# A new recorded order for the first part of a Performer-attention and FNet-mixing kernel: other engines and other PSUM banks for the same instructions

## The chip, the core and the metric

The kernel runs on one core of one Trainium2 chip. The core has five engines, each with an instruction queue that is worked off strictly in order: TensorE (PE) for matmuls and transposes, VectorE (DVE), ScalarE (ACT), GpSimd (POOL), and SyncE (SP), which here issues nearly all DMA transfers. They meet through semaphores: an instruction at the head of a queue waits until its semaphores have reached their values, and everything behind it on that engine waits with it. The metric is the time of one execution in microseconds (us); lower is better.

## The reference, cut to what matters

Inputs: q, k, v of 8 batches x 8 heads x 576 positions x 64, omega (128 x 64), and two weight matrices, 512 x 2048 and 2048 x 512 (given as 64-bit floats).

```
phi(x) = exp(x @ omega.T - |x|^2/2 - max(...)) / sqrt(128)      # per position, 128 features
kv     = sum over positions of phi(k) (x) v ;  z = sum of phi(k)
attn   = (phi(q) @ kv) / (phi(q) @ z + 1e-6)                     # 8 x 576 x 512 after joining the heads
u      = attn + Re(FFT over positions and channels of attn)
out    = u + relu(norm(u) @ w1) @ w2                             # norm: mean 0, variance 1 per row
```

## The kernel before, in words

**Two parts.** The first part does attention, the Fourier mixing, the narrowing of the weights to 32 bits, and the first 512 of the 4608 rows of the final two-matrix block ("plain" rows). The second part does the other 4096 rows in 8 blocks, with a Strassen-like scheme of 7 x 7 products (lines 1495, 1646 and 1892). The change touches the first part alone.

**The steps of the first part.** Work is written as Python generators that yield `Step` objects, one per group of instructions on one engine.

- `attn(n)` (32 of them, one for a pair of heads): `transposed` (L564) turns k and q on PE in groups of 4, 4 and 1 blocks into a PSUM bank each, `evicted` copies each group to SBUF on ACT (L580) or DVE (L578); `pairs_of` (L658) projects on omega into a pair of banks, for 4, 1 and 4 blocks; `softmax` takes row maxima on DVE (L601) and exponentials on ACT (L618); the KV step (L692) sums k features times v, `keep` copies the result (L706 DVE or L708 ACT); the q features are turned (L564 again, evicted the same way); the ND step (L739, L747) multiplies them by kv; then the quotient is formed on DVE (L756, L757, L768), or the last of it on ACT (L764, ten instructions in place of one).
- `mix(b)` (8, one per batch): `folds` adds and subtracts halves on DVE or POOL (L795 to L831), PE multiplies by the tables (L851, L861, L901, L912), `residual` and `summed` add the result to x (L945 to L963), which goes to DRAM through SP.
- `narrow(i)` (32): one 128 x 512 piece of weights, on ACT or POOL (L491, L489), then DVE (L494 to L501), then POOL or DVE (L507).
- `plain_of(j)` (4): L1167 and L1190 on PE, with `hidden` (L1151 DVE or L1153 ACT) between; `w2_parts` prepares sums of the second weight matrix on POOL or DVE (L1332).
- `warm` issues six dummy matmuls (L535) that depend on no load; `first` turns omega (L543), which is loaded through ACT's queue (L447).

**What sets the order.** `Listing.run` holds the next step of every generator. It does not decide anything itself here: the string `PICKS` has one character per step. `picked` reads a character as a number and splits it by 36: the remainder says which of the waiting steps comes next, the quotient which of the engines that the step allows does it (capital letters are the second engine). The string `BANKS` has one digit per PSUM request: the bank, or the first of a pair. The steps are emitted in that sequence, and each engine's queue is that sequence cut to the engine:

```
            other, n = next(picks, (None, None))
            for item in todo if n is None else [todo[n]]:
                got = self.start(*item[2:], other, item[0] + item[2].bias if n is None else None)
...
        if self.taken < len(self.given):
            i = int(self.given[self.taken])
            return i, max(t, *self.banks[i : i + n])
```

The cost figures in the steps are a plan's and have no influence on the chip once a character is given for each step. `PICKS2` and `BANKS2` do the same for the second part.

## Time and profile before

| what | value |
|---|---|
| median of 3 runs (lowest to highest) | 1133.14 us (1130.63 to 1134.68) |
| the profiled execution's own time | 1134.51 us |
| its span in the trace | 1132.7 us |
| granted TensorE clock, mean | 1.00 |
| last instruction of the first part on PE, first of the second part | 421.6 us |
| PE busy | 1116.3 us, 99% |
| DVE, ACT, POOL busy | 77%, 48%, 38% |

How to read it: a busy PE is one with a matmul somewhere in its pipeline, so short waits hide in its 99%. What a wait costs is seen better from one matmul's start to the next one's. In the views that list waits, `ACT e L618 <- DVE nmx L601` means that ACT stood idle ahead of the exponentials of L618 until DVE's maxima of L601 were there. A time window is given as start:end from the span's start.

### The profile page before, as it was taken

The numbers are of one execution on the slowest core, as the hardware profiler recorded it, in microseconds if no ns is written. First come the engines' busy times: TensorE is split into PE (matmuls) and PEld (weight loads), VectorE is DVE, ScalarE is ACT, GpSimd is POOL, SyncE is SP. The second block draws the span as 40 slices with busy tenths as digits, with TensorE's granted clock in tenths as the row PEclk, the third lists the DMA queues.
The fourth block names the chain that finished last, engine by engine and source line by source line (L and its number), as shares of the span: only waits on it lengthen the run. The fifth ranks groups of instructions, "written<-read, shape, count | busy, mean of one in ns | idle before, by whom it ended". The sixth has DMA issues, their size and how long they took to land.

```text
span 1132.7 us, 34265 instructions
## 1 busy us (share of the span) xinstructions
PE 1116.3 (99%) x13643; PEld 1040.2 (92%) x13643; DVE 867.6 (77%) x1732; ACT 541.7 (48%) x1644; POOL 428.1 (38%) x438
## 2 busy tenths in 40 slices
PE   8999999999999999999999999999999999999998
PEld 7778888879868778999999999999999999999998
DVE  6999899987576655796787778678678678678666
ACT  7888898856535216614424424424423522522311
POOL 2443443654573214613612710710720630540361
PEclk9999999999999999999999999999999999999999
DMA  7856766565763238797797798797698698798576
GB/s 242 224 177 180 224 181 215 170 206 170 222 196 126 93 92 284 211 314 246 227 339 232 219 329 241 213 326 258 202 323 264 210 281 298 214 268 293 184 223 205
DMA packets 187966, 258.30 MB, mean 228 GB/s; under 512 B 52384, under 2 KB 83360, under 8 KB 187808
## 3 DMA queue, kind: packets, MB, share of 16 engines
q1 hardware_dynamic: 187312, 255.85, 73.1%
q8 instruction: 109, 1.79, 0.7%
q14 instruction: 49, 0.40, 0.1%
q10 hardware_dynamic: 496, 0.26, 0.1%
HBM read 212.27 MB, written 47.97 MB: 230 GB/s over the span
## 4 chain that ended last, share of the span: by engine, by line
PE 89%; DVE 4%; ACT 3%; DMA 2%; issue 1%; SPq 0%; DVEq 0%; ACTq 0%
PE banks L1892 28%; PE banks L1495 28%; PE banks L1167 5%; PE banks L658 5%; PE banks L1190 5%; PE banks L564 4%; PE banks L1646 4%; PE banks L692 3%; PE banks L739 2%; PE banks L901 2%; ACT e L618 1%; PE banks L851 1%; DMA unT<-turned 1%; DVE nmx L601 1%; PE banks L861 1%
## 5 line engine op out<-in xcount | busy, mean ns | idle before, releaser
L1892 PE MATMUL banks<-wl,sums 128*128 128x128 f32 x1792 | 218.9, 275 | 0.7 <-DVE sums L1460 0.7
L1892 PEld LDWEIGHTS banks<-wl,sums 128*128 128x128 f32 x1792 | 209.3, 192 | 1.1 <-DVE sums L1460 0.9
L618 ACT ACTIVATE e<-banks,nmx 128x128 f32<-128x128 f32 x576 | 164.3, 423 | 24.3 <-DVE nmx L601 23.7
L1460 POOL TENSOR_TENSOR hid<-hid 128x512 f32<-128x512 f32 x97 | 127.0, 1314 | 119.1 <-ACT hid L1552 66.5
L1892 PE MATMUL banks<-wl,hid 128*128 128x128 f32 x1344 | 170.6, 275 | 0.6 <-DVE part L1870 0.4
L1892 PEld LDWEIGHTS banks<-wl,hid 128*128 128x128 f32 x1344 | 160.2, 192 | 1.1 <-DVE part L1870 0.6
L601 DVE TENSOR_REDUCE nmx<-banks 128x8 f32<-128x1024 f32 (+1 forms) x96 | 89.4, 952 | 18.3 <-PE banks L658 14.2
L1495 PE MATMUL banks<-rx,wx 128*128 128x128 f32 x672 | 88.8, 275 | 0.0
L1865 ACT ACTIVATE s<-banks 128x128 f32<-128x128 f32 x112 | 30.8, 277 | 113.2 <-PE banks L1892 97.7
L1495 PEld LDWEIGHTS banks<-rx,wx 128*128 128x128 f32 x672 | 81.8, 192 | 0.0
L658 PE MATMUL banks<-om,kqT 64*64 64x128 f32 (+1 forms) x2088 | 78.7, 275 | 2.2 <-ACT kv L708 1.9
L1538 DVE TENSOR_TENSOR hid<-banks,s 128x512 f32<-128x512 f32 x72 | 49.7, 691 | 38.9 <-PE banks L1495 36.9
L658 PEld LDWEIGHTS banks<-om,kqT 64*64 64x64 f32 (+1 forms) x2088 | 64.3, 138 | 13.1 <-issue 3.6
L1870 DVE TENSOR_TENSOR part<-banks,s 128x128 f32<-128x128 f32 x112 | 32.1, 288 | 50.0 <-PE banks L1892 48.8
L1520 ACT ACTIVATE s<-banks 128x512 f32<-128x512 f32 x65 | 38.7, 596 | 59.7 <-PE banks L1495 58.6
L1167 PE MATMUL banks<-unT,w 128*128 128x128 f32 x512 | 65.4, 279 | 1.7 <-DVE qeT L578 1.7
L507 POOL TENSOR_TENSOR w<-w,raw 128x512 f32<-128x512 f32 x28 | 37.7, 1356 | 77.6 <-DVE raw L501 77.6
L1442 DVE CUSTOM_DVE_ANT_0 hid<-banks,s 128x512 f32<-128x512 f32 x63 | 43.6, 692 | 27.5 <-PE banks L1495 25.2
L1167 PEld LDWEIGHTS banks<-unT,w 128*128 128x128 f32 x512 | 60.2, 192 | 4.5 <-issue 2.3
L1460 DVE TENSOR_TENSOR hid<-hid 128x512 f32<-128x512 f32 x91 | 61.1, 712 | 3.8 <-ACT hid L1598 3.8
L1518 DVE TENSOR_TENSOR s<-banks,hid 128x512 f32<-128x512 f32 x70 | 48.4, 691 | 19.0 <-PE banks L1495 16.7
L1941 POOL TENSOR_TENSOR ur<-ur,part 128x512 f32<-128x512 f32 x21 | 26.8, 1281 | 95.4 <-ACT part L1934 91.6
(200 smaller groups left out, 2387.4 us busy)
## 6 DMA issues: line engine op xcount, KB each, us to landing
wl<-w2l SPq DMA_DIRECT2D x392, 256.0 KB
wx<-w1l SPq DMA_DIRECT2D x126, 256.0 KB
raw<-in_moe_w_ch_dram SPq DMA_DIRECT2D x32, 512.0 KB
kq<-in_k_dram SPq DMA_DIRECT2D x32, 288.0 KB
kq<-in_q_dram SPq DMA_DIRECT2D x32, 288.0 KB
vd<-in_v_dram SPq DMA_DIRECT2D x32, 288.0 KB
u<-us SPq DMA_DIRECT2D x36, 256.0 KB
ur<-us SPq DMA_DIRECT2D x36, 256.0 KB
```

Source lines behind the costliest of these rows:

```text
L564: nc.tensor.transpose(ps[:, (j - j0) * 128 : (j - j0 + 1) * 128], src(j), ident[:])
L601: nc.vector.tensor_reduce(nmx[:, :, 0:num], pps[:, :, 0 : MF * num].rearrange("p b (c m) -> p b c m", m=MF), axis=AX.X, op=ALU.max, negate ...
L618: nc.scalar.activation(out=e[:, c + (i if num == 1 else 0), :], in_=pps[:, i, MF * c : MF * c + MF], func=AF.Exp, bias=nmx[:, i, c : c + 1],)
L658: nc.tensor.matmul(pps[cols, c, MF * m : MF * m + MF], lhsT=kqT[rows, j, cols], rhs=om2[rows, :],)
L1167: nc.tensor.matmul(hp[:, 0:TP], lhsT=w1[:, dc, 128 * fc : 128 * fc + 128], rhs=unTs[key][:, dc, :], start=(dc == 0), stop=(dc == NDC - 1),)
L1190: nc.tensor.matmul(yp[:, 0:DM], lhsT=hs[fc][:, 128 * i : 128 * i + 128], rhs=w2[:, fc, :], start=(fc == 0), stop=(fc == NFC - 1),)
L1460: eng.tensor_tensor(out=o, in0=l, in1=r, op=op)
L1495: nc.tensor.matmul(ps[:, P * f : P * f + P].rearrange("f (b q) -> f b q", q=Q), lhsT=left[:, P * f : P * f + P], rhs=right, start=start an ...
L1518: nc.vector.tensor_tensor(out=s[:], in0=ps, in1=cell_of(addend, f, t), op=ALU.add)
L1538: nc.vector.tensor_tensor(out=o, in0=ps, in1=kept[saved][:], op=ALU.add)
L1646: nc.tensor.matmul(cell.rearrange("f t (b q) -> f t b q", q=Q), lhsT=w[:, d, col : col + 128], rhs=right[:, :, d].rearrange("f (t b) q -> ...
L1892: nc.tensor.matmul(ps[:, 0:128], lhsT=left[:, f], rhs=wls[j, i, n][:, f], start=start and f == 0, stop=(f == 3), skip_group_check=True,)
```

## The change

The strings `PICKS` (1853 choices) and `BANKS` (470 requests) of the first part are replaced; no other line is touched.

```
 PICKS = (
-    "40e0f03eafdaegebg3NbcbeefdcOdeccfgdb37ghj0gjj7hlP79aj7ik97i8S7efhjffeHldffiehdjfdOihgihidaKedbhhciff"
...
+    "410ff4bdcegdge0efcgbfcb9eacg38agdahQiRg3gjPihae887ggdhaPg8gbfaahej88khfef9eajih0Pdbkdmebejf8e7b9dea9"
...
 BANKS = (
-    "0102346120164024306243643016204164024320632462014021604606245062345042604670426420340267407231640260"
...
+    "0123460254604623465402560723462040260762407646206124016404267023406214260456274260340265042673502642"
...
```

The instructions are the same in kind and number, apart from those that change engine. Read off the two built programs:

| work | engine before | engine after |
|---|---|---|
| evictions of turned k, q and features (L580 ACT, L578 DVE), instructions | ACT 221, DVE 67 | ACT 232, DVE 56 |
| `keep` (L708 ACT, L706 DVE) | ACT 20, DVE 12 | ACT 26, DVE 6 |
| quotient (L764 ACT, ten each; L768 DVE) | ACT 4, DVE 28 | ACT 9, DVE 23 |
| first step of `narrow` (L491 ACT, L489 POOL) | ACT 24, POOL 8 | ACT 28, POOL 4 |
| `hidden` (L1153 ACT, L1151 DVE) | ACT 44, DVE 20 | ACT 36, DVE 28 |
| first folds (L795) | DVE 11, POOL 5 | DVE 8, POOL 8 |
| sums of `w2_parts` (L1332) | DVE 10, POOL 34 | DVE 18, POOL 26 |

On PE the 498 steps of the first part are the same, in another order. The first rows of PE's queue are, before: dummy matmuls (L535), four transposes of the first k (L564), omega's transpose (L543), five transposes, `pairs_of` for 4 and 1 blocks, four transposes of the second k, `pairs_of` for the last 4 blocks. After: omega's transpose, the dummy matmuls, nine transposes of the first k and q, `pairs_of` for 4, 1 and 4 blocks, nine transposes of the second k and q. PE changes its tiling (whole array, rows, halves, quarters) 167 times before and 173 times after. At the end of the part the last mixing step of the last batch stands ahead of the last eight L1190 steps before, and ahead of the last five after; SP's last store of that batch's rows then stands behind the copy that waits for its mirrored rows (L988). The second part's queues are the same, instruction by instruction.

More of the change, by code (lines that the diff above doesn't have):

```diff
@@ L67 @@
 PICKS = (
-    "40e0f03eafdaegebg3NbcbeefdcOdeccfgdb37ghj0gjj7hlP79aj7ik97i8S7efhjffeHldffiehdjfdOihgihidaKedbhhciff"
-    "ecgOfeejdfdPdeeedgifdffdefd8aiii88jhd8jP8b99i8e8jcddghjgheiifcOcdciieicgPgdefJcdghbkededfgcRbggb79ij"
-    "8hi7hjafN9Haj9gfffeg8eif8hcej1jccc7ehidbhffLigebfbe6766gggfcbjahj9Ofghhjj8dQkkgT6jghff8de6dUjfhbgegh"
-    "cefhafjUf8jgciSjOckkhjakkaeikggjlioklnhSgodoXON7l7l6nnj9icadc97cibf98ejH88a7edhMlhkmjjaQVijihkkfplSm"
-    "okliljjilVaghVhnmljkmpjkhhnmkimlgglmbjpjjQ9d9alafhhdjlaMdjback0j766k7lh4g896ck6gkki77gij5ijhgj6dimni"
@@ L73 @@
-    "3ndjgi6Kc4jldlKikbkaijLhf75dcjlmklk36ci45jciekajkkkk5kihokeaeoLaioNlencidonbSiljjcmjjkboijTUUhgcfkik"
-    "hiflkmeFF99nol5m8jT7naabda89Rbj97ecdl8cjilOgifkQb4acahg57ebbgabgdjkdTkk6eceebb5f9dg4R6ce486ggg6egfhh"
-    "fg4g9egf5cbdhgPRhhcgjhggejigibLmHnbedijj6NOb7biihi9bgihMkaffPa8cijdhbdghbaeibNefffacjicigifi99975ih5"
-    "jgj8699ajfg6g7fgefd65bO6Kalkkgd5jgjikagfldliPJpeoaeeefgdejadgilgScljiii5e65k56kl57k7j67S9lilk9gliih6"
-    "ffkgec4fg4dbgg7fedaiP5gfbheefilddddddeghg9kbfncgghcfkkafkagGngb65p5Hopoj4bhoanbelli68bjjl5b7dlhighhi"
@@ L78 @@
-    "lflhpkgiWomjknmmmkimnjbjhn9jkmFKkfFgedccff6Wf7idUVhi8Th3fogbqp8fgmkeSdjna7ckenoghmnmffnjeo79q6547oa4"
-    "nlkpd7aceonnc8blSVicilbhmjim8fh7SnnIl5mUkfjgfhhfhihg8ghfbS4kjf83j4lllb79jei8mnkblfnmmiolpilOUi9Mh5l5"
-    "pmnaem79jjVmkbblek5iji9a9kffTgjikhiShfgjafhgfigh4g50PPP0ba5Pdh9dghdK77hgfdcbg8OO988jMehefibjjkellfcc"
-    "PcdhQMihfQcffbKCf82b3c98cbcdcd6a299efgddbJaGQQbefLa9ecf74gg986HRgf9idg8kQeheff7be6ff2e5cc8fbcgdKP8f8"
-    "9hN9Lc999bddcHcNb7Oc9effegd7ibhQeQ8haf7ccghhlUikhHW5lWmm5dkMQGM71fS6d1gdb99747ifddhIfdhhdhfdbihgiljn"
@@ L83 @@
-    "gWgijgg93ekKl8kEhIIbT3jjKgkb9k9eTfhkhlje34m49974iG66h68faHe6e7a79982975aI94a39c8cM8b4aa7ab984fge8eLM"
-    "98b86ce8PbFPc9cbe6cKPf3a9b94fIdIQeJKbd876eJPdc5fNb7ffbf9JSS8RiLa4a7gPbajfgg8gdfhg2i2787Hf6OcdIN5d3LH"
-    "accd46ddeKK72dJc7bbaa4bb9a9bc7c0777dghhdf7Bfddebd76ff1fddIe9949438686bc6aca85348dHcG7a5be957b55d1544"
-    "9Gc1F5a9a68446344584584E59189970955888574443113301110"
+    "410ff4bdcegdge0efcgbfcb9eacg38agdahQiRg3gjPihae887ggdhaPg8gbfaahej88khfef9eajih0Pdbkdmebejf8e7b9dea9"
+    "Habc9jb88fjj9hhUhb7hdclMhRh7b7k8Kbcb7cbbbdhdeaebbh78dbbe79iaaeaQccfee9e7hhce8bdMbbdfgcfbhkdf8Mfbecib"
@@ new lines @@
+    "ji9eagSdddjhiagjffedifedjla918jki9ch9ejMggbaeelm6f9bihjdl78hdJjfP9gkhfccbijgfdkbl6d7fae9d7fkfhgideaj"
+    "hbg9efiekjePg6eiciaie9M6dglikhOKMicafbm6ifdejeii9lckkNij7dhijfhabgaecad7ffOba7cdgc8Pcfjdfeibdafcbc7c"
+    "gKiaijgieMbaci9jifgQlbeQfRgibg9hkgkejfhcd0hme7hc4abefi7gdLm8ke9kbabc8bl5hdffahOcjchhef6db5dkiji8c9eO"
+    "O8ame77jgibeeQ8g9cO377hhgikjfcfill9mg7gle9ld7bQlhldcll3e7gfif9d8eTdeedclf8hh8kV8dhcjhejdcaIbfd9fOhG8"
+    "Shb9igfdNg88MddaehfacebfbcbbcPb9bf85aaadGhffhP4h5gea7bhjjhkR88kkk9aeheibchg697ghggc6agaae49ah86geMdb"
@@ new lines @@
+    "akd9fgchfQge9bbMfjiSddckl9hLReifUUibai9fjceOdjebhafi6jhdie7acg9jbMOfc6eb98hf9R6kk489ejeg896eef6c8hgf"
+    "NNfg85lgi7ld8mbhh8hTgh8dgcmeiampjhOld9hmadhi5fdbaONegghiecQikfi5589bgbd9f9ifacfeiadmfhfiihk9NlikkRa9"
+    "4bd4gadcae9fcbiehbdMbfcNcdPbfcefcegdd68M7dcc9hckfKh4fdddhacl9mmi9ijgcafkh85K6fajjdfjgg778iHl7hmghio6"
+    "phNoO6heelh9peeghkgokdhflhfelmgbfek74cfg8lc8m6eNidTicjT3h8eTgaUi7ghhcigRPcoRiigefgj7lfbjU8Wj47efe6i9"
+    "fT4akgdd84khij9fb6achjj7eegf8Ode7gfg4ckfbijbj6nhmmgckf38jlg9lmmbOkd9elgahL9ihWlnkg7mlilmn8enn5abpqId"
@@ new lines @@
+    "mllceiecQjhafkkbkjOie6kgdeTe8dgc0QgcdOOdd4fMFMdbf3bb98GcNOdcg5dbd7aK5RSiNRd7Qc6gf9ddMfbb7K8eLfcbNcae"
+    "aagdfaOdLeON53ebceg9f7JMdcdb4bcKa9a785d78f07e832J7N5e796L5d76eGcI29e6L6cgb6fc7hIge8KJ5Icdb6cabdLc677"
+    "bb677afG5aPIJaffffdOeO6ab455cd9acbc4a8cb8bffaa9e59Lfaj4Hchaijj95abcIgafdQg8PR3heb9bba7eJ76edb397eMdb"
+    "acfafg51fa6c9iaeMhj8iOa6dTT2S6bc5d6666gffbgfabe6gcfHch9Hfab4ffJg9ad1ddbJb7N45f7HaMbc55cH9ddd4cM95747"
+    "a6GNddIab9H0G7454cb44Jafbbbc9a3aMf95geL3dca6gdaQgejj8h19Rc7OPbbe8i8cghcd90g68Mhib19c7eh9Dag7d67i3I0f"
@@ L87 @@
+    "6d8F9fcff9d8G8b90beae49eaffacaa6cb667bb8251343448954798abc83b3F477aaaE98aaa2a7Da9G049b56bbG59387K841"
+    "766438014353154A6392869265903131651442144453022210000"
 )
 BANKS = (
-    "0102346120164024306243643016204164024320632462014021604606245062345042604670426420340267407231640260"
-    "4524016460620240674206206415704602546064320143607264506402346234062732017426042106147026740260462462"
-    "0410652604632452017205467402624060404256174302642060245016745202642016420634520520650162505605260250"
@@ L93 @@
-    "1675602501605204672016204567627450264102316742067460260462045642062637230724672402630145420640106240"
-    "5264023026731602454230412046450416725730620424670121726154305610207453"
+    "0123460254604623465402560723462040260762407646206124016404267023406214260456274260340265042673502642"
+    "0162014246406420140214604630240632456724072360346241064206342064726345723046013240364270164206402420"
+    "6406152470426701457043762462042040642630271432602464206723146702604236240120164261426416243615246214"
@@ L95 @@
+    "5671362416124606245234026540742360642360152706432637026426130724062042150634527240612345042623452042"
+    "6064502670425142605246430264670645107243620642601453726140152606706420"
 )
```

## The prediction, made before the run

> **What bounds the kernel now.** I read the stretches of the span first. Columns: length, then busy time of PE, its weight loads, DVE, ACT and POOL, then clock, DMA share and rate.

> ```profile
> 0.00:27.00 27.00, 23.67 (x375) 20.38 (x375) 17.74 (x29) 19.51 (x68) 6.83 (x14) 1.00 0.79 239
> 27.00:72.00 45.00, 42.67 (x943) 36.25 (x943) 42.51 (x90) 41.10 (x153) 18.06 (x17) 1.00 0.66 186
> 72.00:117.00 45.00, 42.70 (x969) 36.80 (x970) 41.96 (x99) 37.91 (x134) 17.06 (x19) 1.00 0.71 213
> 117.00:172.00 55.00, 53.13 (x1228) 47.17 (x1227) 51.15 (x106) 48.51 (x179) 25.00 (x22) 1.00 0.68 197
> 172.00:222.00 50.00, 50.00 (x1120) 43.27 (x1122) 47.35 (x106) 44.09 (x156) 24.16 (x24) 1.00 0.62 194
> ```

> From 27 to 222 us DVE is busy 93 to 95% of the time and ACT 84 to 91%: both run a step behind PE. Next, PE's starts. I took the spacing of each kind of matmul from the timeline (112 ns for L1167, 109 for transposes, 429 for L1190), and for each of the 498 PE steps the shortest usual time to the next one: 0.437 us for four transposes, 0.874 for four blocks of projection, 1.024 for KV, 1.166 for ND, 1.92 for each of L851's, 1.41 or 0.71 for a mixing step, 0.893 for L1167's group, 1.719 for L1190's, some 0.125 for a change of tiling. With the dummy matmuls this adds up to 394.4 us. The second part starts at 421.6, so PE loses 27.2 us. Where: a step with 10 us of PE work ahead of it starts 4.9 us late, with 20 us 6.1, with 60 us 11.5, with 100 us 16.5, with 200 us 22.1. The second part (711 us) is L1495 and L1892 at 112 ns each, with under 2 us lost in all; its queues are unchanged. So the prize is at most 27 us, and 16 of it lie in the first 117 us.

> Then the chain of work that ended last, between 40 and 100 us (start, length, what):

> ```profile
> 45.61 4.63 ACT e L618 x18
> ...
> 54.04 1.24 DVE nmx L601
> ...
> 57.16 2.14 ACT x L764 x10
> ...
> 71.49 4.97 DMA raw<-in_moe_w_ch_dram
> ...
> 87.97 2.63 ACT e L618 x10
> ...
> 90.83 2.06 ACT e L618 x8
> ```

> The chain leaves PE for ACT's exponentials and DVE's maxima: there PE is fed just in time. Last, the timeline of PE in the opening:

> ```profile
> 1.04 2.93 PE L535 MATMUL banks<-ur 128*128 128x128 f32 x12 [1.04 <-DVE ur L449]
> 3.96 1.08 PE L564 MATMUL banks<-ident,kq 128*128 128x128 f32 x4
> 4.84 0.42 PE L543 MATMUL banks<-ident,om 128*128 128x128 f32 x1
> 5.05 1.04 PE L564 MATMUL banks<-ident,kq 128*128 128x128 f32 x5
> 6.02 1.39 PE L658 MATMUL banks<-om,kqT 64*128 64x128 f32 x20
> 9.52 0.66 PE L564 MATMUL banks<-ident,kq 128*128 128x128 f32 x4 [2.11 <-DMA kq<-in_k_dram]
> ```

> The dummies fill the time until k lands, at 213 ns each; matmuls are spaced by half that from 5.7 us on, where the granted clock becomes 1.00. PE waits once, 2.1 us for the second k.

> **The change, part by part.** All sums are against the profiled execution (span 1132.7, its own time 1134.5); the median of the runs shown is 1133.1, and I carry the differences over to that.

> *Opening: a loss.* Omega's transpose now heads PE's queue and waits for its load, whose last semaphore update is at 4.02 us; the twelve dummy matmuls (six calls) stand behind it. Omega turned at 4.05, dummies 12 x 0.213 = 2.56 until 6.83, nine transposes at 0.213 until 8.75 (3.96 to 6.0 before). ACT's first eviction goes from 5.08 to 7.93. I followed the new queues by hand from there. First projection 8.75 to 9.65, its maxima on DVE 9.98 to 11.1 (1.13 each), then the maxima of the other two groups to 12.6, two evictions at 0.6 to 13.8. ACT has exponentials from 11.25 (0.25 each): 4, 2, 4 and 4, to 14.75. The first KV step needs the last of these: 14.9, against 12.98 before, with 0.2 us more PE work done ahead of it: 1.7 us later. The second k (landed 9.47) costs no wait now. Walked on to 18 us of PE work, ACT never stands idle, PE has lost 7.2 us, and the deficit against before is 1.2 us, since before also waits there. Bounds: 0.3 (the clock is granted as early as before, and the transposes take half the time) and 2.5 (cold through the projections too). I take 1.2, where the walk ends. [...]

> *Tiling changes: +0.6.* 173 in place of 167, at 0.09 to 0.2 us each. Bounds 0.5 and 1.2.

> *Balance, 20 to 100 us of PE work: -2.6.* With the rows' spacing (0.25 an exponential, 0.48 ACT and 0.60 DVE for an eviction of four, 1.13 for maxima, 0.74 DVE or 1.96 ACT for a quotient), the steps emitted in this stretch cost DVE 80.3 us before and 77.7 after, ACT 74.5 and 77.5. DVE is the fuller engine there by the stretches, with only 5.5 us idle in 90, so I let the stretch shrink by DVE's 2.6 us. That holds if ACT, with 11 us idle in these 90 us, takes its 3 us more out of that idle time. Bounds: -7 and +3 (the last is the second rival).

> How tight each engine is can be put in one number: the work that ACT's queue holds up to the step that a PE step needs, less the PE work ahead of that PE step. Before, its highest value is -3.5 us for ACT and -2.2 for DVE; after, -1.4 for ACT (at 40 to 50 us) and -4.6 for DVE. The tight place moves from DVE to ACT.

> *Balance, 100 to 200: -3.0.* DVE 94.6 to 88.0, ACT 87.1 to 89.3, and both numbers fall: DVE from -3 to -8 and below, ACT from -6 to -13 before, -4 to -12 after. PE lost 5.6 us here; 1.4 of it is one stall at 130.9 that the chain calls "issue" and that I leave. Of the other 4.2 I take 3.0. Bounds: 0 and -4.2.

> *After 200: -1.5.* PE lost 5.1 us, 1.9 of it once, at 331 us:

> ```profile
> PE banks L1167 <- DVE qeT L578: 1.7, 1, 1.7
> ```

> By the same rows DVE has some 13 us less to do in the whole part (321 to 308), so I take most of this one. Bounds: +1 and -4.

> *The seam: 0.* The last mixing step now ends some 8.5 us ahead of the second part (17 before). From it follow an ACT copy (0.4), DVE's combination and sum (2.2), three pairs of SP issues (1.2 each); the last store goes out some 3 us ahead of the seam and lands about with it. The second part's first ACT and DVE steps wait for these stores, but DVE must first do L1203, which can't end before 0.8 us after the seam. What hides the store is that; if SP is 3 us later than I count, it costs up to 3 us, since banks of L1495 are emptied by the same DVE. POOL (174 us of work in the first part) takes 9 more folds' pieces and 8 fewer sums, and stays far from a limit.

> Sum: 1.2 + 0.6 - 2.6 - 3.0 - 1.5 = -5.3, so 1133.1 - 5.3 is about **1128**; I say 1128.

> **The rivals.**

> *The gain is eaten up: 1133.* The new order removes the waits that can be read off, and others of the same size appear, because PE, ACT and DVE together have no more slack than before (ACT and DVE together 154.8 us before and 155.2 after between 20 and 100 us). For it: these sums. Against it: the slack from 100 on. Time: opening and tilings +1.8, half of the DVE terms gone and the rest -2: 1132 to 1134.

> *ACT becomes the bound: 1138.* The chain shown above already runs through ACT's exponentials, and the list of waits has ACT waiting 4.1 us in 4 places for raw weights from DRAM, which holds up everything behind them in its queue; ACT now narrows 28 pieces in place of 24 and forms 9 quotients in place of 4 (1.96 us in a row each). If its idle time in the 20 to 100 stretch stays at 11 us, the stretch gets 3.0 longer; in the next ACT's 2.2 more cancel the gain. With 1.8 from opening and tilings this is +3 to +5, 1138 with the opening at its upper bound. It decides where ACT's idle time there falls by less than 3 us. For it: a highest value of -1.4 is closer than any before. Against it: in the walk ACT went without a gap from 11.25 to beyond 25 us, which the old order never did.

> **How the numbers follow.** Forecast (faster, 1124 to 1130): 0.45. Gain eaten up (1130 to 1136): 0.30. ACT as the bound (1136 to 1142): 0.25. What a measurement of this kernel can tell from no change is about 0.3%, 3.4 us, so these are also the chances of faster, same and slower. The range leaves out about 0.1 on each side: 1123 (the -7, -4.2 and -4 don't all come true at once) to 1139.

> **What would show it right or wrong.** Right: the dummy matmuls start near 4.2 and the first KV step near 15; DVE's share falls and ACT's rises in 27 to 222; PE's lateness at 100 us of work is 15 or less, and the second part starts near 416. Wrong: a start of the second part at 421 or later; ACT no busier than 91% while PE waits for L618, L580 or L708; the second part's first L1495 groups waiting for ACT or DVE behind the last stores; or a PE stall of several us that one bank, named in advance and still held, causes.

## The result, and the profile after

| what | before | after |
|---|---|---|
| median | 1133.68 us (18 runs, 1130.12 to 1137.63) | 1137.72 us (18 runs, 1132.35 to 1140.48) |
| ratio, 95% interval | | 1.0034 (1.0021 to 1.0048) |
| the profiled execution, its span | 1134.5, 1132.7 | 1137.4, 1135.2 |
| second part starts on PE | 421.6 | 422.0 |

The change makes the kernel slower by 4.0 us (medians; 0.34%). A second set of 12 runs on another chip gave 1135.71 against 1133.11, ratio 1.0016 (1.0002 to 1.0029). Two executions are left out of what follows, one of the first experiment's kernel (2273 us, twice the others' time) and one of e10 (1609 us, granted clock 0.65); the first kernel's profiles come from later runs.

The stretches of the span, after; columns as before (length, then busy time of PE, its weight loads, DVE, ACT and POOL, then clock, DMA share, rate):

```profile
0.00:27.00 27.00, 21.12 (x355) 18.70 (x356) 16.11 (x29) 18.50 (x61) 4.98 (x13) 1.00 0.77 226
27.00:72.00 45.00, 42.74 (x924) 36.11 (x926) 40.43 (x84) 42.86 (x162) 12.71 (x11) 1.00 0.69 195
72.00:117.00 45.00, 41.95 (x959) 35.66 (x954) 38.54 (x91) 39.42 (x141) 26.77 (x28) 1.00 0.68 199
117.00:172.00 55.00, 53.20 (x1256) 47.33 (x1256) 50.18 (x101) 48.15 (x178) 29.51 (x27) 1.00 0.65 204
172.00:222.00 50.00, 50.00 (x1054) 43.17 (x1054) 45.14 (x102) 45.98 (x165) 25.25 (x28) 1.00 0.70 207
```

The work did move as the diff says: from 27 to 222 us DVE falls from 183.0 to 174.3 us and ACT rises from 171.6 to 176.4. In the first 27 us everything is lower: PE got 355 matmuls done where it had done 375.

The chain of work that ended last, 40 to 100 us, after (start, length, what):

```profile
47.11 2.96 ACT e L618 x11
...
57.34 1.28 PE banks L851 x8
...
59.95 1.03 PE banks L658 x32
...
73.54 0.96 PE banks L692 x52
74.50 0.80 issue
```

Before, much of it ran over ACT's exponentials and DVE's maxima up to 94 us. Now, from 53 us on, it runs over PE's own steps for long stretches (from 81 to 90 us over DVE and POOL): PE is fed in time there. But pieces called "issue" stand in between, and PE's list of waits from 14 us to the end of the part says how much they are (engine, line, what it waited for: total, times, longest):

```profile
PE banks L658 <- issue: 1.8, 1, 1.8
PE banks L747 <- issue: 1.8, 1, 1.8
PE banks L692 <- issue: 1.4, 2, 0.8
PE banks L658 <- ACT kv L708: 1.2, 1, 1.2
```

With 0.5 more at L739 that is 5.5 us in which PE waited for nothing that the profile shows. The same list of before has one such entry:

```profile
PE banks L739 <- issue: 1.4, 1, 1.4
```

The 1.7 us for `qeT` at 331 us is gone. So are most of the other waits: without that one and without "issue", before's list adds up to 4.9 us and this one to 1.8.

The timeline of PE in the opening, after:

```profile
4.11 0.45 PE L543 MATMUL banks<-ident,om 128*128 128x128 f32 x1 [4.11 <-DMA om<-in_omega_dram]
4.35 2.73 PE L535 MATMUL banks<-ur 128*128 128x128 f32 x12
6.91 1.15 PE L564 MATMUL banks<-ident,kq 128*128 128x128 f32 x9
8.20 2.28 PE L658 MATMUL banks<-om,kqT 64*128 64x128 f32 x36
10.41 1.09 PE L564 MATMUL banks<-ident,kq 128*128 128x128 f32 x8
```

Here the clock was granted at 6.91, just ahead of the transposes, and the first KV step came at 14.16 (12.98 before). In the second profile of the same kernel it was granted at 9.93: the transposes took 2.13 us in place of 1.15, and the first KV step came at 15.34.

By the prediction's measure (start of a PE step less the PE work ahead of it), before and after: 4.9 and 6.4 us late with 10 us of work ahead; 6.1 and 8.1 with 20; 11.5 and 13.0 with 60; 16.5 and 19.0 with 100; 22.1 and 23.8 with 200; 27.2 and 26.9 at the end. So in this pair the loss is there by 15 us of work and stays until before's stall at 331 us evens it out. One profile of each is little: in the changed kernel's second profile the second part starts at 425.0. The other 2.1 us of this pair lie in the second part (707.2 and 709.3 us from its first to its last matmul), whose queues are the same. Over all profiles of this study its length was 706.6 to 709.4. PE's listed waits in it add up to 1.3 us before, 2.9 in this profile and 1.4 in the changed kernel's second one, whose second part took 707.3: this is scatter of its own, no effect of the change.

### The profile page after: what moved, and what is told of

It is laid out like the page before. It is cut to its first block, busy times and chain, and to the rows that moved or that the text cites. A ratio compares the mean times of both kernels' runs of the same rounds, so it can differ in the third digit from the quotient of the medians.

```text
span 1135.2 us, 34315 instructions
## 1 busy us (share of the span) xinstructions
PE 1115.7 (98%) x13643; PEld 1039.5 (92%) x13643; DVE 862.6 (76%) x1710; ACT 557.7 (49%) x1707; POOL 431.1 (38%) x442
## 3 DMA queue, kind: packets, MB, share of 16 engines
q8 instruction: 108, 1.77, 0.6%
## 4 chain that ended last, share of the span: by engine, by line
PE 92%; DMA 4%; DVE 2%; issue 1%; ACT 1%; POOL 0%; SPq 0%; DVEq 0%; ACTq 0%
PE banks L1495 28%; PE banks L1892 27%; PE banks L564 5%; PE banks L1167 5%; PE banks L658 5%; PE banks L1190 5%; PE banks L1646 4%; PE banks L692 3%; PE banks L739 3%; DMA unT<-turned 2%; PE banks L851 2%; PE banks L901 2%; DMA wl<-w2l 1%; PE banks L861 1%; PE banks L912 1%
## 5 line engine op out<-in xcount | busy, mean ns | idle before, releaser
L1892 PE MATMUL banks<-wl,sums 128*128 128x128 f32 x1792 | 219.1, 275 | 1.3 <-DVE sums L1460 0.9
L1892 PEld LDWEIGHTS banks<-wl,sums 128*128 128x128 f32 x1792 | 209.3, 192 | 1.9 <-DVE sums L1460 1.3
L618 ACT ACTIVATE e<-banks,nmx 128x128 f32<-128x128 f32 x576 | 164.1, 434 | 25.9 <-DVE nmx L601 25.5
L1892 PE MATMUL banks<-wl,hid 128*128 128x128 f32 x1344 | 170.7, 275 | 1.6 <-DMA wl<-w2l 1.2
L1892 PEld LDWEIGHTS banks<-wl,hid 128*128 128x128 f32 x1344 | 160.3, 192 | 2.2 <-issue 1.5
L601 DVE TENSOR_REDUCE nmx<-banks 128x8 f32<-128x1024 f32 (+1 forms) x96 | 89.6, 952 | 17.2 <-PE banks L658 15.4
L1495 PE MATMUL banks<-rx,wx 128*128 128x128 f32 x672 | 88.8, 275 | 0.0
L658 PE MATMUL banks<-om,kqT 64*64 64x128 f32 (+1 forms) x2088 | 79.0, 275 | 4.2 <-issue 1.8
L1495 PEld LDWEIGHTS banks<-rx,wx 128*128 128x128 f32 x672 | 81.8, 192 | 0.0
L658 PEld LDWEIGHTS banks<-om,kqT 64*64 64x64 f32 (+1 forms) x2088 | 64.2, 138 | 16.0 <-issue 6.3
L1167 PE MATMUL banks<-unT,w 128*128 128x128 f32 x512 | 65.6, 279 | 0.0
L1941 POOL TENSOR_TENSOR ur<-ur,part 128x512 f32<-128x512 f32 x21 | 26.9, 1287 | 96.7 <-ACT part L1934 96.6
L1167 PEld LDWEIGHTS banks<-unT,w 128*128 128x128 f32 x512 | 60.4, 192 | 3.2 <-issue 2.7
```

The costliest lines, as they stand in the source:

```text
L601: nc.vector.tensor_reduce(nmx[:, :, 0:num], pps[:, :, 0 : MF * num].rearrange("p b (c m) -> p b c m", m=MF), axis=AX.X, op=ALU.max, negate ...
L618: nc.scalar.activation(out=e[:, c + (i if num == 1 else 0), :], in_=pps[:, i, MF * c : MF * c + MF], func=AF.Exp, bias=nmx[:, i, c : c + 1],)
L658: nc.tensor.matmul(pps[cols, c, MF * m : MF * m + MF], lhsT=kqT[rows, j, cols], rhs=om2[rows, :],)
L1167: nc.tensor.matmul(hp[:, 0:TP], lhsT=w1[:, dc, 128 * fc : 128 * fc + 128], rhs=unTs[key][:, dc, :], start=(dc == 0), stop=(dc == NDC - 1),)
L1495: nc.tensor.matmul(ps[:, P * f : P * f + P].rearrange("f (b q) -> f b q", q=Q), lhsT=left[:, P * f : P * f + P], rhs=right, start=start an ...
L1892: nc.tensor.matmul(ps[:, 0:128], lhsT=left[:, f], rhs=wls[j, i, n][:, f], start=start and f == 0, stop=(f == 3), skip_group_check=True,)
```

## The experiments

Three theories stood at first. **O**, the opening: PE starts 3 us later, and what ACT and DVE lose there is never made up. **A**, ACT became the bound. **S**, the seam delays the second part. Others joined them later, each explained where it is first expected; **C** is that chance makes the difference, by where the clock's windows and the transfers of PE's code fall in an execution. A window is a stretch of 3.41 us: in the profiles of before and after the two changes of the granted clock lie 1126.40 us apart, 330 times 3.413, and in e1_look two stretches of 3.41 us at 0.50 start 122.88 us apart, 36 times 3.413. In the diffs below a row is a group of PE's queue; a kernel that changes the order was made by writing `PICKS` and `BANKS` anew, so that only the rows named move.

### The opening undone alone, twice

```
 # the changed kernel, PE's queue
+L535 dummy matmuls x6
 L543 omega's transpose
-L535 dummy matmuls x6
 L564 nine transposes of the first k and q
```

> The changed kernel, with its first two PE steps exchanged: the dummy matmuls stand ahead of omega's transpose again, all else as changed. Theory O (the opening costs the time: PE starts 3 us later, and what it lost by 15 us of work, 2.4 us in the profiled pair, is never made up): first KV step near 12 us (14.2 in the changed kernel, 13.0 before), a step with 20 us of PE work ahead starts some 6 us late (8.1 changed, 6.1 before), and the time falls by 2 to 2.5 us from the changed kernel's, to 1.5 to 2 above before. Theory A (ACT, which has more to do, sets the pace from 20 to 100 us): the head start is lost again by 60 us of work, lateness there 12.5 to 13, time 3 to 4 above before. Theory S (the seam: the second part is 2 us longer because the last stores come later): as A for the time, second part still 713.

> The same kernel as with the dummy matmuls first, for a profile at the full clock. Theory O: clock granted between 3.8 and 7.2 us, ACT's first eviction near 5.1 to 5.5 (7.4 in the changed kernel), so ACT and DVE have some 2.4 us of head start; a step with 20 us of PE work ahead starts about 6 us late, one with 100 us 16.5 (8.1 and 19.0 changed); second part starts near 419 to 420. The part of the gain of 5 us that the first part doesn't show must be in the second, whose queues are the same: theory S', the second part's length follows from when its DMAs start, 711 or less here.

> The changed kernel with the dummy matmuls ahead of omega's transpose, once more, on the same chip as the changed kernel itself: its first runs were 5 us below the changed kernel's, its one usable profile 0.6 above. Theory O (PE's late start costs the time): 4 to 5 below the changed kernel here too. Theory C (what differs is chance: where the windows of the clock and the code transfers of PE fall in a run): within 1.5 of it, and a wider spread than the kernel before.

> The changed kernel, nothing edited. Theory O: 4 above the kernel before, as measured. Theory C: the medians move by 1 to 2 from chip to chip. In the profile: PE's waits for nothing shown (issue) at the same places of its queue as in the other profiles of this order (matmuls 220, 980, 1360, 1740 and 2629), 4 to 6.5 us in all; in the kernel before one of 1.5.

Measured: 1132.37 us against 1132.66 before (ratio 0.9998, 0.9985 to 1.0012), and on another chip 1133.31 against 1133.11 (1.0009, 0.9992 to 1.0027), with the changed kernel at 1135.71 beside it. By the medians two neighbouring steps in PE's queue carry the whole loss: against before, the changed kernel stood 4.0 higher and this one 0.3 lower; on the chip where both ran, 2.6 and 0.2 higher. So 4.3 and 2.4 us come back. The 2.4 alone is not clear of noise: resampling the 12 executions of each gives -1.0 to 3.9. Part of the noise can be told from the record, which has the granted clock of each execution. With those alone where it was 0.999 or 1.000 (9 and 7 of 12) the difference is 3.1 (1.2 to 4.4): 1135.6 after, 1132.5 here, 1132.8 before (30 of 35). The profile of the second set, opening:

```profile
4.16 0.45 PE L543 MATMUL banks<-ident,om 128*128 128x128 f32 x1 [0.19 <-DMA om<-in_omega_dram]
4.40 2.02 PE L564 MATMUL banks<-ident,kq 128*128 128x128 f32 x9
6.35 2.28 PE L658 MATMUL banks<-om,kqT 64*128 64x128 f32 x36
8.75 1.59 PE L564 MATMUL banks<-ident,kq 128*128 128x128 f32 x9
```

The transposes start 2.5 us earlier than after the change and the first KV step comes at 12.3. ACT's first exponentials start at 8.8 instead of 10.7 (first line: after; 11.9 in its second profile):

```profile
10.67 5.28 ACT L618 ACTIVATE e<-banks,nmx 128x128 f32<-128x128 f32 x20 [1.86 <-DVE nmx L601]
8.82 5.28 ACT L618 ACTIVATE e<-banks,nmx 128x128 f32<-128x128 f32 x20 [1.70 <-DVE nmx L601]
```

A step with 20 us of work ahead is 5.8 late, with 100 us 15.0, and the second part starts at 418.4. The profile taken in between shows the other end of this kernel's scatter: 1138.0, the second part at 423.5, with the clock taken back twice (0.50 from 11.57 to 14.98 and from 134.45 to 137.87 us). That scatter is part of theory C; that it would bring the two kernels within 1.5 of each other is not borne out by the medians, and where the clock was kept the data speak against it.

### Order and engines apart

```
 e2: order and BANKS as changed, the 142 steps that changed engine as before
 e3: order and BANKS as before, the 142 steps on the changed engines
```

> The changed kernel's order and PSUM banks, with every one of the 142 steps that changed engine given back to the engine it had before. Theory A: the loss goes, time within 1.5 of before. Theories O and S: the time stays 3 to 5 above before; with DVE's 13 us of work back, more likely 5 than 3. The second part by S 713, by the others 711.

> The kernel before, its order and banks, with the 142 steps on the engines that the change gives them. Theory A: 2 to 4 us above before, lost between 20 and 100 us of PE work, PE waiting for ACT. Theories O and S: within 1.5 of before, perhaps a little below it, since DVE has 13 us less to do and the stall at 331 us (PE for DVE's evicted features, 1.9 us) gets shorter. The second part by S 711.

Measured: 1151.69 (ratio 1.0166, 1.0148 to 1.0185) and 1187.16 (1.0479, 1.0459 to 1.0499). No theory had expected this. Order and engines fit only together: with the changed order and the old engines PE waits 7.0 us for `kqT` from DVE in five places; with the old order and the new engines once 7.9 us for `qeT` from ACT, and the clock is taken back five times (its mean over the execution is 0.987). These two say nothing for or against A; they say that 142 single choices, each worth tenths of a microsecond by its duration, leave the kernel 19 and 54 us above the one before in a queue that was not ordered for them.

### The seam undone alone

```
 # e6: the changed kernel; its last 62 steps in the sequence of before, engines as changed
```

> The changed kernel, its last 62 steps put into the sequence that they have in the kernel before (engines as changed): the last mixing step stands some 17 us ahead of the second part again, and SP's last store of the batch ahead of the copy that waits for its mirrored rows. Theory S: the second part takes 711 (713 in the changed kernel) and the time falls by 2, to 2 above before. Theories O and A: time 3.5 to 4.5 above before; the second part differs from run to run by itself.

Measured: 1137.87 against 1132.66 (1.0039, 1.0025 to 1.0052); second part 708.7. S falls.

### The same edit in the kernel before

```
 # e5: the kernel before, PE's queue
+L543 omega's transpose
 L535 dummy matmuls x6
 L564 four transposes
-L543 omega's transpose
 L564 five transposes
```

> The kernel before, with omega's transpose put ahead of the dummy matmuls, the same edit the other way round (the nine transposes of the first k and q then stand together); all else as before. Theory O: the loss is the same here, 3 to 5 us above before. Theory W (the wait of 2.1 us for the second k, from 7.4 to 9.5, takes it up in this order): 0 to 1.5 above before.

Measured: 1136.08 against 1133.91 (1.0014, 0.9999 to 1.0029). By the ratio it costs 1.6 us here (-0.1 to 3.3, so no change is just possible; 2.2 by the medians): less than O said, at or above the upper end of what W said. The first KV step comes at 14.7 instead of 13.0; at 120 us of work this profile is level with before again.

### What of the opening costs: late clock or late start

```
 # e8: the changed kernel
 L543 omega's transpose
-L535 dummy matmuls x6
 L564 nine transposes
 L658 first three projections
+L535 dummy matmuls x6

 # e13: the changed kernel
+L535 six dummy matmuls more
 L543 omega's transpose
 L535 dummy matmuls x6
 L564 nine transposes
```

> The changed kernel, with the dummy matmuls taken from behind omega's transpose to behind the first three projections: PE still starts at 4.1 us with omega and is granted the clock as late as in the changed kernel (7 to 10 us), but the first nine transposes don't wait 2.6 us for the dummies. Theory O-delay (what costs is that the evictions, maxima and exponentials start late): ACT's first eviction near 5.1 to 5.5, time within 1.5 of the kernel before. Theory O-clock (what costs is the late grant: transposes and projections at half rate): as the changed kernel or worse, 3.5 to 5 above before.

> The changed kernel, with six dummy matmuls more (12 records) ahead of omega's transpose; the other six stay behind it. PE is busy from 1.0 us on, the clock is granted between 3.8 and 7.2 us, but the nine transposes of the first k and q still stand behind dummies (1.3 to 2.6 us of them). Theory O-clock (the late grant costs the time): as with the dummy matmuls first, 0 to 1 above the kernel before. Theory O-delay (that the transposes, and with them ACT's and DVE's first work, stand behind the dummies costs it): 1.5 to 3 above before.

Measured: e8 1137.80 against 1133.91 (1.0030, 1.0010 to 1.0050); e13 1136.94 against 1133.99 (1.0019, 1.0004 to 1.0034). Each has one of the two causes, and each is nearly as slow as the changed kernel. In e8 nothing but omega's transpose stands ahead of the transposes, but they and the projections run at half rate, since the clock came at 9.18:

```profile
4.38 2.13 PE L564 MATMUL banks<-ident,kq 128*128 128x128 f32 x9
6.44 3.57 PE L658 MATMUL banks<-om,kqT 64*128 64x128 f32 x36
```

In e13 the clock came at 5.98, but the transposes stand behind dummies until 6.54:

```profile
4.48 2.23 PE L535 MATMUL banks<-ur 128*128 128x128 f32 x12
6.54 1.15 PE L564 MATMUL banks<-ident,kq 128*128 128x128 f32 x9
```

Either way ACT's first exponentials come at 9.8 and 10.3 us, 1 to 1.5 later than with the dummies first. O-delay is right for e13, O-clock for e8; neither alone is the cause. Not all of the loss need be the opening's own: in both, 6 of 12 executions had a granted clock of 0.998 or less, and in the other 6 the medians stand 2.0 (e8) and 1.2 (e13) above before's of the same kind.

### PE's waits for nothing shown: where they are

By the page's DMA queues, instructions come in pieces of 16 KB, 1.77 MB in 108 packets (packets, MB, share; of after):

```profile
q8 instruction: 108, 1.77, 0.6%
```

13643 matmuls with a weight load each, in 108 pieces, are 126 matmuls a piece. In the changed order the five waits stood at matmuls 220, 980, 1360, 1740 and 2629 of PE's queue (in its second profile at the last four of them and at 4151), whole multiples of 126.75 apart to within two matmuls, and each ended 1.4 to 1.6 us after a piece's transfer had ended. That these pieces are PE's is inferred from this; in the first part 59 transfers pair off with 59 such places.

```
 # the kernel with the dummy matmuls first, PE's queue
 L658 first three projections
+22 matmuls 64x65 (e10), or six more dummy matmuls 128x128 (e11)
 L564 transposes of the second k and q
```

> The kernel with the dummy matmuls first, and 22 small dummy matmuls more (44 records of 64x65) ahead of the second k's first transpose, where PE waits for that k anyway (1.2 us). All that follows on PE stands 44 matmuls further along in the code. Theory F (PE's waits without a shown cause are waits for its own code, which comes in pieces of some 127 matmuls with their weight loads, and a piece lands some 2.4 us after its transfer starts): the places at which PE waits move by 44 matmuls to the front, none is left at 2629; by the traces' lengths of such pieces and delays of transfers, 2 to 3 us more are lost, so 2 to 3 above the kernel with the dummy matmuls first. Theory N (the waits belong to instructions, not to places in the code): they stay at the same instructions, time as that kernel's within 1.

> The same with six whole dummy matmuls (12 records, 1.3 us at the full clock) in the place of the small ones: PE is busy while it waits for the second k, so no clock window from 8 to 12 us stands empty. Theory C: the clock is not taken back at 9 to 12 us in any run, the spread of the times gets narrower and the median 0.5 to 1.5 lower than the kernel with the dummy matmuls first. Theory O: no change, since that wait is not on the path.

Measured: e10 1135.30 (1.0017, 0.9999 to 1.0036), e11 1135.06 (1.0020, 1.0002 to 1.0039), before 1133.11. In e10 the longest wait is again the one at matmul 2629 of the queue, 2.9 us, but it now strikes L658 where it struck L747: it stayed at its place in the code while the instructions moved past it. In e13, 12 records further along, it strikes L739. So F is right about what these waits are (the expectation's "none is left at 2629" meant the old count of instructions). Its price is not shown: e11, moved by 12 only, lost as much as e10. C's hope for e11 failed: PE was kept busy through the opening, but in its profile, with a mean of 0.996, the clock was taken back at 91 and 136 us, at the waits for code there. In 8 of its 12 executions the granted clock was 0.998 or less; the other 4 have a median of 1133.2, near that of the kernel before.

### Taking the longest of these waits away

```
 # e12: the kernel with the dummies first, PE's queue; no other queue changes
 L692 KV
+L1167 (fc 4)
 L658 projections
+L1167 (fc 5)
 L739, L747 ND
...
 # e14: the kernel before, PE's queue; no other queue changes
 L692 KV
 L658 projections
 L1167 (fc 4)
+L1167 (fc 5)
 L739, L747 ND
```

> The changed kernel with the dummy matmuls first, and with two of the L1167 groups (fc 4 and 5 of the first plain tile) moved on PE alone, 17 and 19 groups forward, so that they stand among the KV and ND steps that fill PE's code from matmul 2500 to 2627; engines' other queues are the same, some PSUM banks differ. Theory F (PE waits for its code there, because it gets through that piece in 2.9 us while the next one takes up to 5 us from being asked for to being there): the piece lasts 5 us, the wait at matmul 2629 (2.0 to 2.5 us in five profiles of this order) falls to 0.6 or less, the clock isn't taken back at 131 to 138 us; 1.5 to 2.5 below the kernel with the dummy matmuls first, so 1.3 to 2.3 below the kernel before. Theory N (the wait isn't the code's): within 1 of the kernel with the dummy matmuls first.

> The kernel before, with one more L1167 group (fc 5 of the first plain tile) moved forward on PE alone, next to the one (fc 4) that stands in the same piece of code there; all other queues the same. Theory F: the wait at matmul 2629 (1.5 us in the profile of before) falls below 0.7; 0.5 to 1.5 below the kernel before. Theory N: within 0.5.

Measured: 1136.70 and 1137.44 against 1133.99 (1.0024, 1.0010 to 1.0038; 1.0022, 1.0006 to 1.0039). The wait at 2629 is gone in both, as F says, and both are slower than the kernels that they were made from (e12 by way of the kernel before). PE's waits of e12, 100 to 150 us, show what came in its place:

```profile
PE banks L739 <- DVE x L768: 1.5, 1, 1.5
PE banks L739 <- ACT kqT L580: 1.0, 1, 1.0
PE banks L692 <- ACT qeT L580: 0.4, 1, 0.4
```

These lines suggest that the wait for code lay beside work of ACT and DVE that PE would have waited for anyway, and that the moved groups pushed ND, and with it the quotient, back; no run shows it apart. e14 has a cost of its own besides: the group moved there waits 1.1 us for ACT's exponentials (`PE banks L1167 <- ACT e L618`), a wait that it did not have in its old place. Between 100 and 140 us of PE work e14's profile loses 6.2 us where before's loses 4.2.

### Two splices of both orders

```
 e9: the order of before up to 290 us of planned PE work, the rest as changed
 e4: the opening of before up to its first KV step, the rest as changed
```

> The kernel before up to 290 us of planned PE work (some 75% of the first part), and from there what is left in the changed kernel's order, engines and banks. If the gain after 200 us that the traces show (PE loses 3.0 us there instead of 5.1, the 1.9 us wait for DVE's evicted features at 331 us gone) is real and stays: 2 below before. If the second part takes it back, or other waits do: as before within 1.

> The changed kernel with the whole opening of the kernel before, up to its first KV step on PE, ACT and DVE; from there the changed order, engines and banks (11 banks differ). Theory O (what costs is how late ACT's and DVE's first work starts): ACT's first exponentials at 7.9 us as before (10.3 to 12 in the changed kernel, 8.4 to 8.8 with the dummy matmuls alone moved); the time is 2.5 to 4.5 below the changed kernel, from 1 below to 0.5 above the kernel before. If the rest of the new order brings its own gain beside that (1.2 us between 20 and 100 us of PE work and 2 after 200 in the best profile): 2 to 3 below before.

Measured: e9 1151.51 (1.0156, 1.0132 to 1.0180), with one hole of 10.8 us at the joint, where PE waits for DVE's L1203: it tells nothing of the tail. e4 1136.83 against 1132.67 (1.0036, 1.0022 to 1.0051), against O. ACT's first exponentials are there at 7.3 us, earlier than in any other profile. But PE waits 1.4 us for a load of q at 11.4, which before did not, and at the joint 1.2 us for `kv` from DVE and 1.4 for the quotient, and with 30 us of work ahead it is 10.5 us late, more than the changed kernel (8.8). In this kernel an early start alone was worth nothing. O in its plain form, that the start of ACT's and DVE's work sets the end, does not hold here; how late PE is by 30 us of work does better.

## Why the prediction was wrong

Forecast: 1128, faster. Measured: 1137.7, slower. The time lies within the range, next to the rival at 1138, but not for that rival's reason: that closeness is luck. The prediction's own marks said wrong: the second part started at 422.0 (wrong from 421 on), and PE was 19.0 late at 100 us of work (right up to 15).

| step | forecast | shown by the traces |
|---|---|---|
| opening | +1.2 (0.3 to 2.5) | +2.1 and +2.7 by 20 us of work in two profiles; undoing it gives back 2.4 and 4.3 by the medians |
| tilings | +0.6 | +0.8 (PE work 394.4 to 395.2) |
| balance, 20 to 100 | -2.6 | +0.4; -1.2 where the dummies stand first (best profile) |
| balance, 100 to 200 | -3.0 | -0.8; -0.5 with the dummies first |
| after 200 | -1.5 | -2.1; the wait at 331 us is gone |
| seam | 0 | 0 |

**Two steps failed: the balance terms by most, and the opening.** The column on the right adds up to +0.4 for the first part in the first pair, the forecast to -5.3. Of these 5.7 us the two balance terms are 5.2 and the opening 0.9. The experiments say the same: the sum without its opening term is -6.5, and the kernel with the opening undone stood level with before.

**The opening** failed by its size, and it makes the difference between level and slower. The walk was right on the order of events: the dummies started at 4.35 (said: 4.2), the first KV step came at 14.2 to 15.5 in three profiles (14.9). It went wrong where it ended, at 18 us of work with a deficit of 1.2: I credited the new order with the second k that costs no wait, and took the rest as paid. The traces show 2.4 at 15 us of work and no recovery behind it up to 200. I had also written that ACT goes without a gap from 11.25 on, and used that against the ACT rival. It was evidence against my own sum: an engine without a gap can't catch up a late start. In the first 27 us ACT did 1.0 us and DVE 1.6 us less than before; both are 86 to 95% busy in every stretch from 27 to 222 us.

**The balance terms were mis-sized.** The step that failed is "so I let the stretch shrink by DVE's 2.6 us", and the 3.0 taken from 100 to 200. DVE's relief was real (the stretches show 8.7 us less busy time from 27 to 222), but the stretches did not shrink by it: in the changed kernel the 20 to 100 stretch gained nothing (the column above sums to 0.4, and the second part's 2.1 makes the pair's 2.5); with the dummies first it gained 1.2 in the better of two profiles. PE's lists of waits show what came in its place: the waits for ACT, DVE and loads did fall, from 4.9 to 1.8 us without the one at 331 us, but the waits for PE's own code, which are in no term of the sum, rose from 1.4 to 5.5. That the second ate up the first is a reading of the lists; it stays open, since in e12 and e14 the longest of these waits went and the time did not fall.

**The rivals.** "ACT becomes the bound": the point from which it decides was a fall of ACT's idle time between 27 and 117 us by less than 3 us. It fell by 3.3 (from 11.0 to 7.7; by 3.7 in the second profile), so by its own mark it doesn't hold, though the time is its 1138. "The gain is eaten up": this is nearer to what was found, waits removed and others of the same size in their place, but its time is right only for the kernel with the opening undone, 1132.4 and 1133.3.

The clock: with nearly the same start of PE (4.11 and 4.05) it was granted at 6.91 in one profile of the changed kernel and at 9.93 in the other, where the nine transposes took 2.13 us in place of 1.15. So the start of PE alone did not fix the grant. My two bounds for the opening, 0.3 and 2.5, stood for an early and a late grant; the profiles with the one and the other show 2.1 and 2.7 by 20 us of work.

How a late opening relates to the end, in the profiles and medians (lateness with 30 us of PE work ahead, median against before on the same chip): before 6.8 us, 0; dummies first 6.3 and 7.5, -0.3 and +0.2; e10 7.9, +2.2; e8 8.2, +3.9; after 8.8 and 9.3, +4.0 and +2.6; e5 8.9, +2.2; e6 9.5, +5.2; e4 10.5, +4.2. By a coarser count, good to some 0.3, e13 stands at 7.8, +3.0, e12 at 7.9, +2.7, and e14 at 9.1, +3.5: it has the opening of before, but in its profile, with a mean of 0.998, the clock was taken back from 10.4 to 13.8 us. e11 (6.5, +2.0) doesn't fit. The lateness is that of one profile, the time that of a dozen executions.

**What the granted clock of the executions adds.** Every profile of 0.998 or less shows a window or more at half rate behind the first grant (136.22 to 139.63 us in the changed kernel's second profile, 0.998; two in e1_look, 0.997); those of 0.999 and above show none until the last 3 us (from 1132.11 in before, from 1133.31 in after), but for one in e2 (309.81 to 313.2). Of the 122 executions of the kernel before whose clock is on record, 95 stand at 0.999 or 1.000, with a mean of 1133.1 us, and 27 at 0.998 or less, with 1135.9. In the comparison on one chip the executions at 0.998 or less have nearly one median in all three kernels: 1136.8 before, 1136.8 after, 1137.1 with the dummies first (5, 3 and 5 executions). There the opening told the kernels apart only where the clock was kept. In the first comparison 6 of the changed kernel's 18 executions stand at 0.998 (median 1139.9; the other 12: 1136.3), so part of its 4.0 may come with lost windows; for before's executions of that comparison the clock is not on record. A window of 3.41 us at half rate (nine transposes took 2.13 us in place of 1.15) can by my estimate itself cost PE no more than half of it, 1.7 us, so the rest belongs to the waits around it; no run separates them.

**What stays open:** what ate up the balance's gain, and why a deficit of 2.1 to 2.7 us in the traces was worth 4.0 in the medians of one comparison and 2.6 in the other, as far as the clock doesn't explain it. Whether the rest of the new order is worth anything with an opening that fits it is open too: the smallest undo reaches before's time, not less, and no kernel tried beat both.

## What to carry to other kernels

Where two engines behind PE are some 90% busy for two hundred microseconds, the first microseconds can set the end, as the two steps of e1 did here: price a step that is moved to the head of a queue by when the fullest engines get their first work, and carry that delay to the end unless a stretch with real slack follows. Put work that waits for nothing ahead of work that waits for a load. An engine's relief is a gain only where the next wait does not take its place: count the waits that a new order brings, not only those that it removes. A recorded order is one thing with its engines: its halves (e2, e3) and one splice (e9) were slower than either whole, and the other splice (e4) was no better than the changed kernel.

## What the runs showed of the hardware

**The clock was taken back at waits shorter than a window.** The second profile of the changed kernel: two windows of 3.41 us at the wait for code at matmul 2629, the clock granted in each behind its busy times:

```profile
132.81:136.22 3.41, 1.68 (x71) 1.34 (x69) 3.19 (x8) 2.52 (x11) 0.89 (x1) 1.00 0.83 217
136.22:139.63 3.41, 3.41 (x45) 3.29 (x34) 0.77 (x2) 2.51 (x9) 1.29 (x1) 0.50 0.09 35
```

PE was busy for 1.68 of 3.41 us, and the next window ran at half rate (0.50), though the wait for code was of 1.7 us. In the kernel before a window with as little PE work was followed by one at the full clock (9.13 to 12.54, 1.00):

```profile
5.71:9.13 3.41, 1.69 (x23) 1.33 (x21) 1.85 (x3) 1.31 (x4) 0.00 (x0) 1.00 1.05 295
```

So PE's busy time in the window doesn't tell these two cases apart. At the start the clock came behind a window with 2.80 us busy (after) and not behind one with 2.29 (e6).
